# The first idle products of TensorE: 30 of 192 columns in place of 11 of 512

## The chip, the cores and the metric

The kernel runs on one core of a Trainium2 chip. That core has a matrix engine (TensorE, "PE" in the profile, with its weight loads shown apart as "PEld"), a vector engine (DVE), a scalar engine (ACT), GpSimd (POOL) and a sync engine (SP) that only issues transfers. Each engine works through its own stream of instructions; they meet through semaphores. Transfers run on 16 DMA engines. The metric is the device time of one execution in microseconds (us), lower is better.

## The reference

An attention with a decaying state is followed by a two-layer network with the exact GELU. Cut to what matters:

```python
# q, k, v: (4, 8, 768, 64); lam: (8,), one decay for each head
for b in range(nb):                       # blocks of 64 positions
    intra = einsum('bhic,bhjc->bhij', qb, kb) * Dmask[None]
    intra = einsum('bhij,bhjd->bhid', intra, vb)
    inter = einsum('bhid,bhde->bhie', qb * lam_pow[None], kv_state)
    out[:, :, sl] = intra + inter
    kv_state = lam_block * kv_state + einsum('bhsd,bhse->bhde', kb * rev_pow, vb)
...
x = out.transpose(0, 2, 1, 3).reshape(3072, 512)
h = x @ w_in                              # 512 -> 2048
g = 0.5 * h * (1.0 + erf(h / sqrt(2)))
result = g @ w_out                        # 2048 -> 512
```

## The kernel before

The 3072 tokens are worked on in 24 chunks of 128 positions (six positions of the sequence times four batches), and the network in six groups of four chunks, 512 tokens each. All products are in bfloat16 with float32 sums.

The order of TensorE's work is written out by hand. The kernel first issues all constants, loads and the start of the attention. Then a loop over the six groups issues the network's blocks (`mlp_blocks`), and a sorted list of due times (`todo`) places the attention's steps for later chunks between these blocks. So TensorE's stream is one fixed sequence without loops: every product stands in it as a pair of instructions, a weight load and a matmul, and there are 2619 such pairs.

In that sequence two kinds of stretches alternate. The network's blocks have long products: L518 (the first layer, up to 512 columns), L414 (the second layer, done by sums of halves as in Strassen's scheme, 256 columns) and, in the first group, L531. Between them lie the visits to the attention (`pair_visit`): `begin_answers` (L314, the states), `ask` (L279, scores), `ask_products` (L290, new state products), `end_answers` (L326 values, and L314 again). A visit has products of 64x64 with 64 columns, up to 128 of them in a row. What they need (transposed q and k) comes by DMA transposes that SP issues. The scaling of a visit's output to the network's input `x_t` is done on the vector engine at L333, and the next block of L518 waits for that.

At the very start TensorE has no data. GpSimd issues the loads of k, q and v of the first chunks; the weight columns come through SP. Until k is there, TensorE is given idle products: `keep_warm(n, new, cols)` (L576 to L581) multiplies a zero tile `idle` (memset at L107) by itself n times into a PSUM bank that nobody reads. Each is a weight load of 128 columns and a matmul over `cols` columns. The first call, in the line that the change touches (L595), stands before the first chunk's transposes (L166 in `transposed`); more calls, of 2 to 7 products of 256 columns, stand between the first steps, up to product 120 or so.

Of the kernel before, what the change touches and what calls it, by code (L numbers as in the profile page):

```python
# [15 lines left out]
def kernel(  # L16
# [131 lines left out]
    def bank(shape, dtype, tag, name):  # L148
        return ps.tile(shape, dtype, tag=tag, name=name, bufs=2 if tag in ("sc", "mh", "mo") else 1)
# [426 lines left out]
    def keep_warm(n, new=True, cols=256):  # L576

        if new:
            idle_ps[0] = bank([128, 512], F32, "mo", "idle_ps")
        for _ in range(n):  # L580
            nc.tensor.matmul(idle_ps[0][:, :cols], idle[:, :128], idle[:, :cols], start=True, stop=True)  # L581

    def early(n):
        live[n] = begin(n, early=True)
        return live[n]
# [6 lines left out]
    nc.scalar.copy(w_in_t[:, :, :256], wide_w)  # L592
    make_powers()
    nc.scalar.activation(warm, pos, ACT.Gelu)
    keep_warm(11, cols=512)  # L595
    c = early(0)
    causal(0)
    transposed(c, "k", "mh", copy)
# [266 lines left out]
```

## Time and profile before

| | us |
|---|---|
| median of three runs | 203.96 |
| lowest, highest | 203.42, 206.22 |
| the profiled execution's own time | 203.09 |
| its span (first to last instruction) | 201.3 |
| TensorE busy | 192.3 |
| VectorE / ScalarE / GpSimd busy | 122.5 / 82.7 / 111.3 |

The span is that of the profiled execution; its own time holds 1.8 us more, which lie outside the program's instructions. The page gives TensorE's products at L581 as one group, with the shapes of 512 and 256 columns together:

```profile
L581 PE MATMUL idle_ps<-idle 128*128 128x256 bf16 (+1 forms) x39 | 9.0, 366 | 1.2 <-DVE idle L107 1.2
```

Of these 39 products, 11 are of the first call. Columns of such a row: line, engine, operation, output and inputs, shape, count, then busy us and mean ns of one, then the engine's idle time just before them and what ended it. In the timeline the columns are start, duration, engine, line, operation, and in brackets the idle time before with its releaser; "issue" stands where the engine waited for nothing that the profile shows. In the view of windows they are the stretch, its length, the busy time with the count of instructions that ran in it, the granted clock, the DMA share and GB/s.

### The profile page before, as it was taken

Reading aid. Unit: us, or ns where it says so; the run is one execution under the profiler, and the core shown is the slowest. Engines: PE = TensorE matmul, PEld = TensorE weight load, DVE = VectorE, ACT = ScalarE, POOL = GpSimd, SP = SyncE. Lnnn points to the kernel's source line nnn. Section 1 sums busy time; section 2 is a strip of 40 time slices with the busy share of each in tenths; the row PEclk is TensorE's granted clock in tenths of the full one; section 3 lists DMA queues with packets and bytes.
Section 4 is the critical chain, followed back from the end, with each engine's and each line's share of the span. In section 5 each row is a group of like instructions: output and inputs, shape, how many; then the busy total and the mean of one; then the engine's idle time right before and its main releaser. Section 6 shows DMA issues by size and latency. Waiting matters only on the chain.

```text
span 201.3 us, 5976 instructions
## 1 busy us (share of the span) xinstructions
PE 192.3 (96%) x2619; PEld 141.6 (70%) x2619; DVE 122.5 (61%) x206; ACT 82.7 (41%) x149; POOL 111.3 (55%) x136
## 2 busy tenths in 40 slices
PE   7699999999999999799999999999999999999992
PEld 2378674555884788686488885588884788865881
DVE  3753507863674869594949678649639358341482
ACT  4964564324567313155620164520265510566200
POOL 8999973789968899992592299394400000000000
PEclk9999999999999999999999999999999999999998
DMA  5999999999999999999599779999930001400014
GB/s 113 155 174 176 198 207 200 156 216 152 145 207 136 137 146 134 141 272 145 61 98 140 234 53 118 102 66 115 155 142 3 3 0 61 151 0 3 0 52 156
DMA packets 102761, 24.76 MB, mean 123 GB/s; under 512 B 93264, under 2 KB 99920, under 8 KB 102736
## 3 DMA queue, kind: packets, MB, share of 16 engines
q0 software_dynamic: 81072, 13.38, 100.3%
q1 hardware_dynamic: 21664, 11.02, 27.7%
q8 instruction: 20, 0.33, 0.7%
q14 instruction: 5, 0.04, 0.1%
HBM read 27.27 MB, written 6.29 MB: 167 GB/s over the span
## 4 chain that ended last, share of the span: by engine, by line
PE 58%; DMA 19%; POOL 15%; DVE 4%; issue 2%; POOLq 0%; DVEq 0%
PE h_ps L518 28%; PE r_ps L414 8%; PE p_ps L414 7%; PE q_ps L414 7%; DMA q_t<-in_q_dram 5%; DMA v_t<-in_v_dram 5%; DMA w_out_t<-in_moe_w_out_dram 5%; DMA qT<-q_t 4%; POOL k_t L70 4%; PE s_ps L414 3%; POOL v_dec L160 3%; POOL v_t L70 3%; POOL w_in_t L94 3%; POOL q_t L70 3%; PE o_ps L314 2%
## 5 line engine op out<-in xcount | busy, mean ns | idle before, releaser
L521 ACT ACTIVATE g_t<-h_ps 128x512 bf16<-128x512 f32 (+2 forms) x99 | 57.8, 584 | 73.0 <-PE h_ps L518 73.0
L518 PE MATMUL h_ps<-x_t,w_in_t 128*128 128x256 bf16 (+3 forms) x640 | 87.7, 294 | 0.0
L518 PEld LDWEIGHTS <-w_in_t 128*128 128x128 bf16 x640 | 57.0, 98 | 24.7 <-DVE x_t L333 0.2
L389 DVE TENSOR_TENSOR g_sum<-g_t 128x1024 bf16<-128x1024 bf16 x50 | 34.7, 739 | 15.3 <-ACT g_t L521 15.3
L414 PEld LDWEIGHTS <-g_sum 128*128 128x128 bf16 x400 | 39.0, 98 | 5.1 <-issue 0.5
L160 POOL TENSOR_TENSOR v_dec<-v_t,lam_m 128x512 bf16<-128x512 bf16 x23 | 24.9, 1100 | 27.4 <-PE o_ps L326 16.9
L70 POOL DMA_DIRECT2D v_t<-in_v_dram x24 | 22.1, 919 | 2.2 <-DMA w_out_t<-in_moe_w_out_dram 1.7
L414 PE MATMUL r_ps<-w_sum,g_sum 128*128 128x256 bf16 x160 | 19.1, 272 | 0.3 <-DVE f_x L484 0.3
L73 POOL DMA_DIRECT2D k_t<-in_k_dram x24 | 18.6, 789 | 0.0
L73 POOL DMA_DIRECT2D q_t<-in_q_dram x24 | 18.2, 778 | 0.0
L414 PEld LDWEIGHTS <-g_t 128*128 128x128 bf16 x160 | 15.7, 98 | 2.9
L531 PE MATMUL o_ps<-w_out_t,g_t 128*128 128x512 bf16 x64 | 15.1, 380 | 0.0
L333 DVE TENSOR_TENSOR x_t<-o_ps,lam_q 128x512 bf16<-128x512 f32 x16 | 10.6, 685 | 5.0 <-PE o_ps L314 5.0
L70 POOL DMA_DIRECT2D q_t<-in_q_dram x12 | 10.8, 903 | 2.3 <-DMA w_out_t<-in_moe_w_out_dram 2.3
L70 POOL DMA_DIRECT2D k_t<-in_k_dram x12 | 11.1, 923 | 1.9 <-DMA w_out_t<-in_moe_w_out_dram 1.6
L305 DVE TENSOR_TENSOR sc_m<-sc_ps,cmask_d 128x512 bf16<-128x512 f32 x16 | 10.3, 681 | 0.0
L531 PEld LDWEIGHTS <-g_t 128*128 128x128 bf16 x64 | 5.8, 98 | 6.2
L581 PE MATMUL idle_ps<-idle 128*128 128x256 bf16 (+1 forms) x39 | 9.0, 366 | 1.2 <-DVE idle L107 1.2
L452 DVE TENSOR_TENSOR o_sb<-f_e,p_ps 128x512 f32<-128x512 f32 x5 | 3.4, 687 | 11.0 <-issue 11.0
L414 PE MATMUL p_ps<-w_out_t,g_sum 128*128 128x256 bf16 x80 | 9.6, 273 | 0.0
L414 PE MATMUL p_ps<-w_sum,g_t 128*128 128x256 bf16 x80 | 9.6, 273 | 0.0
L414 PE MATMUL q_ps<-w_sum,g_t 128*128 128x256 bf16 x80 | 9.6, 273 | 0.0
(90 smaller groups left out, 194.2 us busy)
## 6 DMA issues: line engine op xcount, KB each, us to landing
out_dram<-o_sb SPq DMA_DIRECT2D x9, 512.0 KB, 4.5
v_t<-in_v_dram POOLq DMA_DIRECT2D x24, 128.0 KB, 6.0
w_out_t<-in_moe_w_out_dram POOLq DMA_DIRECT2D x4, 512.0 KB, 10.2
w_in_t<-in_moe_w_in_dram POOLq DMA_DIRECT2D x7, 256.0 KB, 7.4
k_t<-in_k_dram POOLq DMA_DIRECT2D x12, 128.0 KB, 6.5
q_t<-in_q_dram POOLq DMA_DIRECT2D x12, 128.0 KB, 6.9
k_t<-in_k_dram POOLq DMA_DIRECT2D x24, 64.0 KB, 4.8
q_t<-in_q_dram POOLq DMA_DIRECT2D x24, 64.0 KB, 5.0
```

Source lines behind the costliest of these rows:

```text
L70: nc.gpsimd.dma_start(raw[n, name], chunk_of(name, n))
L73: nc.gpsimd.dma_start(raw[n, name][:, r::2, :], chunk_of(name, n)[:, r * HP:(r + 1) * HP, :])
L94: nc.gpsimd.dma_start(w_in_t[:, :, f], w_in_r[:, :, f])
L160: eng.tensor_mul(c.v_dec, c.v, lam_m[:, :, None].to_broadcast((128, H, D)))
L305: nc.vector.tensor_mul(w.sc_m[:, hi], w.sc_ps[hi], cmask_d[:, None, None, :].to_broadcast((128, 2, HP, D)))
L333: nc.vector.tensor_mul(x[:, :, :, HALVES[t]], pairs[n].o_ps[t], lam_q[:, :, None, HALVES[t]].to_broadcast((128, HP, 2, D)))
L389: nc.vector.tensor_tensor(gsum[i][:, ks, :], g_t[:, ka + k:ka + k + n4, ta], g_t[:, kb + k:kb + k + n4, tb], op=op)
L414: nc.tensor.matmul(o, left[i](k, slice(u * C, (u + 1) * C)), right[i](k), start=(begin and k == 0), stop=(k == KH - 1), skip_group_check=True)
L518: nc.tensor.matmul(h_ps[:, k, :], w_in_t[:, ki, (kf + k) * 128:(kf + k + 1) * 128], x_t[:, ki, cols], start=(k == 0 and ki == 0), stop=(ki ...
L521: nc.scalar.activation(g_t[:, kf:kf + ks, cols], h_ps, ACT.Gelu)
L531: nc.tensor.matmul(om[io], g_t[:, kf, io * C:(io + 1) * C], w_out_t[:, kf, :], start=(kf == 0), stop=(kf == NK2 - 1))
L581: nc.tensor.matmul(idle_ps[0][:, :cols], idle[:, :128], idle[:, :cols], start=True, stop=True)
```

## The change

One line: the first call of `keep_warm` issues 30 products of 192 columns in place of 11 of 512. That is 5760 columns in place of 5632, and 60 instructions in place of 22. The zero tile, the PSUM bank and the other calls stay as they are; so do the other engines' instructions, every wait and every transfer.

```diff
     make_powers()
     nc.scalar.activation(warm, pos, ACT.Gelu)
-    keep_warm(11, cols=512)
+    keep_warm(30, cols=192)
     c = early(0)
     causal(0)
     transposed(c, "k", "mh", copy)
```

## The prediction

> **What bounds the kernel now.** I began with the page, its span and busy times:
>
> ```profile
> span 201.3 us, 5976 instructions
> ...
> PE 192.3 (96%) x2619; PEld 141.6 (70%) x2619; DVE 122.5 (61%) x206; ACT 82.7 (41%) x149; POOL 111.3 (55%) x136
> ...
> q8 instruction: 20, 0.33, 0.7%
> ```
>
> TensorE is busy for 192.3 of 201.3 us and nothing else comes near, so the time can only change through its idle time, its clock or its amount of work. The work at stake is the idle products, which compute nothing that is used. The last row is for later: 20 packets carry TensorE's instructions while it runs, 0.33 MB / 20 = 16.4 KB each. TensorE issues 2 x 2619 = 5238 instructions (each product has a weight load), which is 262 for each packet.
>
> Second, the list of all waits of TensorE:
>
> ```profile
> PE o_ps L314 <- issue: 1.3, 2, 1.1
> PE idle_ps L581 <- DVE idle L107: 1.2, 1, 1.2
> PE t_ps L166 <- DMA k_t<-in_k_dram: 1.0, 2, 0.8
> PE t_ps L166 <- DMA q_t<-in_q_dram: 0.4, 2, 0.2
> PE r_ps L414 <- DVE f_x L484: 0.3, 1, 0.3
> PE sc_ps L189 <- DVE qT L169: 0.3, 1, 0.3
> PE sc_ps L279 <- DMA qT<-q_t: 0.3, 1, 0.3
> ```
>
> Two things are to be seen. The first real product (L166, a transpose of k) waits 0.8 us for its load, so the idle products in front of it end early. And the longest entry has no releaser at all: "issue" at L314, two pauses deep inside the kernel, 1.3 us in total.
>
> Third, the timeline, at the start (TensorE and its weight loads), and with it the view of the idle tile, restricted to the first 6 us (durations are ns, min/median/max):
>
> ```profile
> 1.19 4.57 PE L581 MATMUL idle_ps<-idle 128*128 128x512 bf16 x11 [1.19 <-DVE idle L107]
> 1.60 0.15 PEld L581 LDWEIGHTS <-idle 128*128 128x128 bf16 x1 [0.28 <-issue]
> ...
> 5.01 0.15 PEld L581 LDWEIGHTS <-idle 128*128 128x128 bf16 x1 [0.28 <-issue]
> 6.61 0.40 PE L166 MATMUL t_ps<-ident,k_t 128*128 128x128 bf16 x4 [0.85 <-DMA k_t<-in_k_dram]
> ...
> L581 PE MATMUL idle_ps<-idle x11: 380/634/634, 1.2 to 5.4; 128*128 128x512 bf16 x11
> ```
>
> From 1.60 to 5.01 lie eight steps of 0.426 us, one product of 512 columns each, so 0.83 ns a column. Only the last product, at 5.4, has the short duration, 380 ns in place of 634: TensorE runs slowly for its first 4 us and reaches its full rate near 5.3 us, while the idle products still run. They are there for that. They end at 5.76 and k arrives for 6.61.
>
> **The change at its own place.** It removes 11 products of 512 columns (11 x 0.426 = 4.69 us at the slow rate) and adds 30 of 192: 192 x 0.83 = 0.160 us each, 4.80 us in all. The difference of 0.11 us, even with every product slow, ends the group near 6.0 in place of 5.76 as the latest, and the wait for k (0.85 us) hides it: I cost it at nothing. If that cover were gone it would cost its 0.11 us. The bounds: no less than nothing, since k's load sets 6.61 whatever TensorE does; at most, a weight load (0.15 us in the rows above) might no longer lie beside a product. Then a product costs 0.31 us until 5.3 (13 of them) and, with half of 0.16 for the fast rate, about 0.23 after that (17 of them, 3.9 us): the group would end near 9.3, 2.7 us late. I take nothing, because each load in the rows starts beside a running product, and 0.15 still fits into 0.160. Total columns and their time being alike, I also leave the moment of full rate at about 5.3.
>
> **What the change moves.** The 19 extra products with their loads are 38 more instructions at the head of TensorE's stream; every later instruction of it stands 38 places further back. No other engine's stream, no wait and no DMA changes. So the places matter where the stream itself is brought in. Here are the two pauses of "issue", and the window counts (x is the number of products started since 0):
>
> ```profile
> 84.18 0.19 PE L314 MATMUL o_ps<-qT,state 64*64 64x64 bf16 x1
> 85.51 0.19 PE L314 MATMUL o_ps<-qT,mid 64*64 64x64 bf16 x1 [1.14 <-issue]
> ...
> 121.77 0.21 PE L314 MATMUL o_ps<-qT,mid 64*64 64x64 bf16 x1
> 122.14 0.19 PE L314 MATMUL o_ps<-qT,state 64*64 64x64 bf16 x1 [0.17 <-issue]
> ```
>
> ```profile
> 0.00:80.05 80.05, 76.21 (x971) 1.00 1.95 166
> 0.00:82.80 82.80, 78.95 (x995) 1.00 1.96 166
> 0.00:84.40 84.40, 80.52 (x1118) 1.00 1.96 165
> 0.00:113.50 113.50, 108.51 (x1483) 1.00 1.84 160
> 0.00:117.15 117.15, 112.16 (x1611) 1.00 1.80 161
> 0.00:119.20 119.20, 114.21 (x1630) 1.00 1.78 159
> 0.00:122.00 122.00, 116.99 (x1757) 1.00 1.77 157
> ```
>
> The pauses come after product 1118 and after product 1757. That is 639 products or 1278 instructions apart, five times 255.6, while a packet carries at most 262. I read this as blocks of 256 instructions (128 products), with an edge after product 1118 and after every 128th on either side, and both pauses as TensorE standing at an edge whose next block has not come. The DMA view of narrow windows (0.2 us in 40 slices of 5 ns; the tall number in the GB/s row is the packet's start) shows the packets, from windows that begin at 83.0, 119.1, 114.9 and 89.9:
>
> ```profile
> GB/s 154 154 462 154 256 282 155 410 180 154 384 230 103 334 154 103 130 107 130 3456 78 206 102 154 78 53 78 128 77 102 102 102 102 128 77 77 102 128 128 154
> q8 instruction: 1, 0.02, 33.2%
> ...
> GB/s 51 26 77 51 102 51 51 128 51 77 26 128 102 102 102 102 102 77 3379 128 51 102 102 128 26 128 77 128 77 102 102 128 77 77 102 128 102 51 128 102
> q8 instruction: 1, 0.02, 47.6%
> ...
> GB/s 410 410 410 0 410 0 1229 1229 0 410 410 410 0 0 3277 410 819 410 410 0 0 0 819 1638 0 410 410 410 0 410 0 0 410 410 410 819 0 0 0 1229
> q8 instruction: 1, 0.02, 47.2%
> ...
> GB/s 410 410 410 819 819 461 435 410 819 410 410 410 0 0 0 410 410 0 410 4096 819 410 410 0 0 410 436 845 0 819 0 410 410 0 410 819 819 410 410 0
> q8 instruction: 1, 0.02, 29.1%
> ```
>
> They start at 83.10, 119.19, 114.97 and 90.00; a share of 16 engines over 0.2 us gives their lengths, 1.06, 1.52, 1.51 and 0.93 us. So the first packet ends at 84.16 and TensorE goes on at 85.51, 1.35 us later; the second ends at 120.71 and TensorE goes on at 122.14, 1.43 us later. Two unlike pauses, one lag: that ties each to its packet.
>
> Why just there? A block seems to be fetched when the stream enters the one before it. The edge before product 1118 is product 990, near 82.25 (five products of L518, some 0.11 us each, before 82.80), and between lies a dense run: 123 products from 82.80 to 84.18, 0.011 us each. From edge to next edge TensorE needs only 1.9 us, and the block took 85.51 - 82.25 = 3.3 us. At the second pause the edge is product 1629, near 119.1, and the block took 122.14 - 119.1 = 3.0 us. Moreover TensorE reached the first of these edges late, held by the vector engine:
>
> ```profile
> 81.86 0.77 PEld L518 LDWEIGHTS <-w_in_t 128*128 128x128 bf16 x8 [0.17 <-DVE x_t L333]
> ```
>
> After the change every edge falls 19 of these products earlier:
> - The edges around the first pause become products 971 (80.06) and 1099 (84.18 - 19 x 0.011 = 83.97). That is 3.9 us for a block that took 3.3: no pause. Gain 85.51 - 84.18 less one step of 0.011, 1.32 us.
> - Around the second they become 1610 (117.05, from the row of 1611 at 117.15) and 1738 (121.56). 4.5 us for a block that took 3.0: no pause. Gain 122.14 - 121.77 less a step, 0.36 us.
> - A third pair comes close: 1482 (113.49) and 1610 (117.05), 3.56 us apart. The same edge of before, 1501 near 113.65, had its packet at 114.97, 1.51 us long; with a lag of 1.4 the block was usable at 117.88, and nobody needed it before 119.1. Moved with its edge it is usable at 117.72 and TensorE stands for 0.67 us. By the blocks of 3.0 to 3.3 us it would not stand at all. I take 0.67, since that row is of the same place with the same transfers around it.
>
> Sum: -1.32 - 0.36 + 0.67 = -1.0 us, with -1.7 as the lower end. What is late next? No other wait of TensorE between 85.51 and 121.77 is in the list of waits, so I expect the time to stay won.
>
> The Trainium skill, "Runtime: NRT & Kernel Launch", section "Instruction fetch mechanics", says that an engine's instructions are refilled in 16 KiB blocks of 256 instructions, the next fetched while the current one runs, and that crossing a block's edge is "mostly hidden". The block size agrees with the 16.4 KB above; "hidden" does not agree with pauses of 1.32 and 0.36 us. By that rule the shift would be worth nothing and the sum would be 0.
>
> **Rivals.**
> *No change.* The pauses come from something that doesn't move with the stream (a wait that the profile doesn't show), or new edges pause as much. For it: "issue" names no cause, and 1278 is two short of five times 256. Against: the equal lag behind two packets. The time stays that of the profiled execution, 203.1. Chance 0.14; the skill's rule of hidden fetches ends here too.
>
> *Slower: a block that comes late in heavier DMA traffic.* The edge at 85.51 (product 1118) had its packet only at 90.00, usable 1.35 us after its end at 90.93, so 6.8 us after its edge. If the block asked for at 80.06 took as long, TensorE would stand 6.8 - 3.9 = 2.9 us where it now stands 1.32: the sum is 2.9 - 1.32 - 0.36 + 0.67 = +1.9 us, time 205.0. It decides from 3.9 + 1.32 = 5.2 us on. Against it: the stream runs somewhat ahead of TensorE, and product 971 lies ahead of the hold at 81.86, so the request should come sooner, not later. Chance 0.13.
>
> *Clock.* The full rate comes only in the next dense stretch. What that costs:
>
> ```profile
> 6.50:8.70 2.20, 1.55 (x21) 1.00 2.42 154
> 8.70:12.10 3.40, 3.07 (x46) 1.00 2.00 167
> ```
>
> TensorE has 4.62 us of fast work in this stretch; at half rate the 5.5 us from 6.61 to 12.1 do 2.75 us of it, so 1.9 us are lost, 204.0 with the gain of 1.0. For it: 0.11 us more of idle products is no guard, and one of the three times of before is 206.22. Against it: the busy stretch is as long as before. The skill's "TensorE: Matmul & The Clock Gate", Part 1, speaks of a free-running window of 3.4 us, by which both kernels would draw this lot alike; one trace can't show that. Chance 0.11. The weight load that no longer fits beside its product (+2.7, less the gain: 204.8) gets 0.02.
>
> **The numbers.** The forecast has chance 0.60. The profiled execution's own time is 203.09 (span 201.3 and 1.8 around it), which gives 202.1; the median of the runs shown, 203.96, lies 0.87 above it, and from there the same sum gives 203.0. I say 202.5. Low: 203.09 - 1.7 = 201.4, taken as 201.3. High: 205.2, which takes in both slower rivals at 204.0 to 205.0 and the no-change case; two of these mishaps together lie above it. Two per cent, 4.1 us, is about what a measurement of this kernel can tell from no change. Faster by that (under 199.9) would need more idle time than the waits of TensorE after 6.61 hold (some 2.7 us together): 0.04. Slower by that (over 208.0) needs two of the mishaps on top of the median, or a far longer slow start: 0.07. Within: 0.89.
>
> **What would show it.** In the profile after: L581 with 30 products at about 0.16 us steps, L166 still waiting for k at about 6.6; no "issue" pause near 84 and 122, counted in products 1137 and 1776; one new pause of up to 0.7 us near 116, after product 1629; the span 200.3. It is wrong if pauses stay at the same products of the dense runs (then the blocks aren't the cause), if a pause of over 1.3 us stands near 84 (then the block's way is slower than I think), or if products after 6.6 still have slow steps (then the clock).

## The result, and the profile after

The changed kernel takes 202.11 us (median of 20 runs) against 204.22 us of the kernel before beside it (20 runs): ratio 0.9909, 95% interval 0.9887 to 0.993, some 1.9 us faster. By the bound of two per cent that is no difference; by its own interval it is one. The profiled execution took 201.49 us, with a span of 199.7 us against 201.3. Ratios here and below leave out an execution over 1.5% above the fastest of its kernel; the times beside them are medians of all.

The page of the changed kernel, its span and busy times, and then the list of TensorE's waits:

```profile
span 199.7 us, 6002 instructions
...
PE 190.8 (96%) x2626; PEld 143.4 (72%) x2638; DVE 121.5 (61%) x206; ACT 82.8 (41%) x149; POOL 111.2 (56%) x136
```

```profile
PE idle_ps L581 <- DVE idle L107: 1.2, 1, 1.2
PE t_ps L166 <- DMA k_t<-in_k_dram: 1.1, 2, 0.9
PE t_ps L166 <- DMA q_t<-in_q_dram: 0.9, 3, 0.5
PE h_ps L518 <- issue: 0.3, 1, 0.3
PE o_ps L531 <- issue: 0.3, 2, 0.2
PE sc_ps L189 <- DVE qT L169: 0.3, 1, 0.3
PE h_ps L518 <- DMA w_in_t<-in_moe_w_in_dram: 0.2, 1, 0.2
```

The entry "o_ps L314 <- issue" of before is gone: neither pause is left. The products of this trace (2626) are 12 fewer than its weight loads (2638), which are complete; the two waits of L531 are the holes of such missing records. So I count weight loads from here on. A load runs one ahead of its product: the first pause of before stands after load 1119.

The pause of L518 is real. The timeline around it, the window count up to it, and the DMA view of the window from 113.5 to 113.7:

```profile
115.15 0.49 PE L518 MATMUL h_ps<-x_t,w_in_t 128*128 128x256 bf16 x3
115.98 0.28 PE L518 MATMUL h_ps<-x_t,w_in_t 128*128 128x256 bf16 x1 [0.34 <-issue]
...
0.00:115.80 115.80, 81.77 (x1630) 1.00 1.75 162
...
GB/s 410 819 1229 410 0 0 410 0 0 819 0 0 0 819 819 0 0 3686 410 0 0 410 410 410 0 410 0 410 0 819 410 410 819 819 410 0 410 0 410 0
q8 instruction: 1, 0.02, 27.4%
```

It stands after load 1630, which to within one is the third edge of the prediction (product 1629). Its packet starts in the 18th slice, at 113.585, is 0.88 us long and ends at 114.46; TensorE goes on at 115.98, 1.52 us later.

At the start the two groups compare as foretold:

```profile
1.19 4.28 PE L581 MATMUL idle_ps<-idle 128*128 128x192 bf16 x30 [1.19 <-DVE idle L107]
6.42 0.40 PE L166 MATMUL t_ps<-ident,k_t 128*128 128x128 bf16 x4 [0.94 <-DMA k_t<-in_k_dram]
...
L581 PE MATMUL idle_ps<-idle x30: 246/364/364, 1.2 to 5.2; 128*128 128x192 bf16 x30
```

Thirty products end at 5.47, and TensorE waits 0.94 us for k. The full rate came near 4.6 us here, where the prediction had left it at 5.3: 22 products had begun by 4.60 and 27 by 5.00.

### The profile page after: what moved, and what is told of

Read it like the earlier page. It is cut to its first block, busy times and chain, and to the rows that moved or that the text cites. A ratio compares the mean times of both kernels' runs of the same rounds, so it can differ in the third digit from the quotient of the medians.

```text
span 199.7 us, 6002 instructions
## 1 busy us (share of the span) xinstructions
PE 190.8 (96%) x2626; PEld 143.4 (72%) x2638; DVE 121.5 (61%) x206; ACT 82.8 (41%) x149; POOL 111.2 (56%) x136
## 4 chain that ended last, share of the span: by engine, by line
PE 77%; DMA 10%; POOL 10%; issue 1%; DVE 0%; POOLq 0%
PE h_ps L518 35%; PE r_ps L414 9%; PE p_ps L414 9%; PE q_ps L414 9%; DMA q_t<-in_q_dram 6%; PE s_ps L414 4%; DMA w_out_t<-in_moe_w_out_dram 4%; PE o_ps L531 3%; POOL w_in_t L94 3%; POOL k_t L70 2%; POOL q_t L70 2%; PE o_ps L314 2%; POOL v_t L70 2%; POOL v_dec L160 1%; PE o_ps L326 1%; PE kv_ps L290 1%
## 5 line engine op out<-in xcount | busy, mean ns | idle before, releaser
L518 PE MATMUL h_ps<-x_t,w_in_t 128*128 128x256 bf16 (+3 forms) x632 | 87.5, 293 | 0.9 <-issue 0.3
L518 PEld LDWEIGHTS <-w_in_t 128*128 128x128 bf16 x640 | 57.0, 98 | 25.5 <-DVE sc_m L305 0.6
L389 DVE TENSOR_TENSOR g_sum<-g_t 128x1024 bf16<-128x1024 bf16 x50 | 33.8, 720 | 16.2 <-ACT g_t L521 16.2
L531 PE MATMUL o_ps<-w_out_t,g_t 128*128 128x512 bf16 x60 | 14.6, 379 | 0.4 <-issue 0.3
L531 PEld LDWEIGHTS <-g_t 128*128 128x128 bf16 x64 | 5.9, 98 | 6.2
L581 PE MATMUL idle_ps<-idle 128*128 128x192 bf16 (+1 forms) x58 | 8.7, 303 | 1.2 <-DVE idle L107 1.2
L414 PE MATMUL s_ps<-w_sum,g_sum 128*128 128x256 bf16 x80 | 9.6, 273 | 0.0
```

Of the source, the lines that this page charges most:

```text
L389: nc.vector.tensor_tensor(gsum[i][:, ks, :], g_t[:, ka + k:ka + k + n4, ta], g_t[:, kb + k:kb + k + n4, tb], op=op)
L414: nc.tensor.matmul(o, left[i](k, slice(u * C, (u + 1) * C)), right[i](k), start=(begin and k == 0), stop=(k == KH - 1), skip_group_check=True)
L518: nc.tensor.matmul(h_ps[:, k, :], w_in_t[:, ki, (kf + k) * 128:(kf + k + 1) * 128], x_t[:, ki, cols], start=(k == 0 and ki == 0), stop=(ki ...
L531: nc.tensor.matmul(om[io], g_t[:, kf, io * C:(io + 1) * C], w_out_t[:, kf, :], start=(kf == 0), stop=(kf == NK2 - 1))
```

## The experiments

Two theories stood against each other. **Blocks**: the time follows where the edges of 128 products fall in the work. **Shape**: it follows what the first idle products are, by their own time or by the clock. The first four runs part them: one moves the stream without the shape, one has the shape without moving, one moves it the other way, one moves it far.

**Moved only.** The first call stays 11 of 512; later calls issue twice as many products of half the width.

```diff
     transposed(c, "k", "mh", copy)
-    keep_warm(3, new=False)
+    keep_warm(6, new=False, cols=128)
     transposed(c, "q", "mo", copy)
     causal(1)
-    keep_warm(2)
+    keep_warm(4, cols=128)
...
-        1: [lambda: keep_warm(7), lambda: outputs(live[1])],
+        1: [lambda: keep_warm(14, cols=128), lambda: outputs(live[1])],
```

> The first idle products as before (11 of 512); the stream moved by the same 19 products by splitting 19 later idle products of 256 columns into two of 128 each, so the columns stay. Theory (blocks of 256 instructions): as the changed kernel, ratio to before 0.991 (0.986 to 0.996); no pause near 84 and 122 us, one of 0.2 to 0.7 us near 116 after product 1629. Rival (the shape of the first idle products, by the clock or their own time): as before, ratio 1.00, with pauses of about 1.3 and 0.4 us at the same work as before.

Measured: ratio 0.9919 (0.9886 to 0.9951), 201.76 us. Its list of waits has no "issue" entry at all; the pauses near 84 and 122 are gone, and the third, expected with 0.2 to 0.7 us, is not there either. The gain is there without the changed line.

**Shape only.** The first call as 23 of 245 columns, and later calls with products merged into 512 columns, so that the count ahead of the work is that of before (the edit is shown against the kernel before).

```diff
-    keep_warm(11, cols=512)
+    keep_warm(23, cols=245)
...
-    keep_warm(3, new=False)
+    keep_warm(1, new=False, cols=512)
+    keep_warm(1, new=False)
...
-        4: [lambda: scores(live[2]), lambda: keep_warm(7)],
+        4: [lambda: scores(live[2]), lambda: keep_warm(3, cols=512), lambda: keep_warm(1, new=False)],
```

> The first idle products as 23 of 245 columns (the change's kind of shape), the stream not moved: 12 products fewer later, where idle products of 256 columns are merged into products of 512. Theory (blocks): as before, ratio 1.00 (0.996 to 1.005), with pauses of about 1.3 us near 84 and 0.4 us near 122, after products 1118 and 1757. Rival (shape): as the changed kernel, 0.991, without pauses there.

Measured: ratio 1.0017 (0.9988 to 1.0046), 203.73 us: the shape brings nothing. Its profile, of an execution of 206.72 us that the ratio doesn't hold, can't stand for that time: there TensorE waits 2.6 us at L484 (last section), and no pause follows at the edge behind it. That this kernel still has the pauses of before thus rests on its time alone.

**Moved back.** The first call as before, the later calls merged as in the run above: 12 products fewer.

> The first idle products as before (11 of 512), the stream 12 products shorter ahead of all the work, by the same merging of later idle products. Theory (blocks): the edges fall 12 products later in the work, so from edge to edge TensorE needs only about 1.4 us near 84 and 1.5 near 121 in place of 2.0 and 2.6; the pauses grow to about 1.9 and 1.4 us, ratio 1.008 (1.003 to 1.012), again after products 1118 and 1757 or so of its own count, which is other work. Rival (shape): 1.00.

Measured: ratio 1.0002 (0.9971 to 1.0032): not the 1.008 expected, and this interval leaves 1.008 out. The places came true, in a profiled execution of 205.58 us that the ratio doesn't hold. The rows after each pause, and the load counts up to them:

```profile
87.75 0.49 PE L518 MATMUL h_ps<-x_t,w_in_t 128*128 128x256 bf16 x3 [1.48 <-issue]
124.78 0.19 PE L314 MATMUL o_ps<-qT,state 64*64 64x64 bf16 x1 [1.14 <-issue]
...
0.00:87.00 87.00, 54.64 (x1119) 1.00 1.93 170
0.00:124.20 124.20, 83.33 (x1758) 1.00 1.76 155
```

Loads 1119 and 1758 again, in work that lies 12 products later: the first pause is now at L518, after the dense run, where before it was at L314 inside it. They last 1.48 and 1.14 us, not 1.9 and 1.4. The executions in the ratio lose less than I worked out; why isn't shown, since none of them has a profile. The ratio also leaves out five of the twelve, 204.95 to 206.34 us, at a granted clock of 0.997 to 1.0. The median of all twelve is 204.28 us, that of all executions of before 203.48. So this run shows where the edges stand, and leaves open what they cost.

**Moved by 59.** The first call as 42 of 134 columns, all later ones split as in the first run.

> The first idle products as 42 of 134 columns, all 28 later ones split into two of 128: the stream moved by 59 products. Theory (blocks): no pauses near 84 and 121; new ones in two other dense runs, about 2 us near 93 after product 1374 of its own count and 0.3 to 1 us near 113 after product 1630; together 2.3 to 3.0 us against the 1.7 of before, ratio 1.004 (1.000 to 1.008). Rival (more and shorter idle products help by themselves): at most the 0.991 of the change, with no pause at 93.

Measured: ratio 1.0131 (1.007 to 1.0191), 207.4 us, worse than expected. The rows after the two pauses in its profile (of an execution of 208.31 us that the ratio doesn't hold), the counts up to them, and the packet of the longer one (window 94.4 to 94.6):

```profile
76.33 0.38 PE L414 MATMUL q_ps<-w_out_t,g_sum 128*128 128x256 bf16 x2 [1.48 <-issue]
97.46 0.61 PE L518 MATMUL h_ps<-x_t,w_in_t 128*128 128x512 bf16 x1 [3.21 <-issue]
...
0.00:75.60 75.60, 50.65 (x991) 1.00 2.02 169
0.00:96.00 96.00, 65.54 (x1374) 1.00 2.04 170
...
GB/s 128 179 128 154 179 179 179 128 102 179 230 102 179 128 179 128 154 179 154 179 129 77 179 128 27 3457 78 77 102 78 128 26 77 27 51 53 26 26 51 26
q8 instruction: 1, 0.02, 44.0%
```

Both follow, to within one, a multiple of 128 counted from 1118: 990 (loads one ahead) and 1374. The pause at 1374 was foretold; that at 990 was not, and the one at 113 did not come. The packet starts at 94.52, when TensorE, busy until 94.25, has already stopped; it ends at 95.93, and TensorE goes on at 97.46: 1.53 us. The half clock behind it, shown in the last section, cost this execution some 2.9 us more (an estimate, half of the 5.8 us there); the executions in the ratio have no profile.

**Moved by 16**, to save the third pause: `keep_warm(27, cols=211)`.

> The first idle products as 27 of 211 columns: the stream moved by 16 products in place of 19. Theory (blocks): the third edge falls three products of L518 later, some 0.3 us, which is the pause that the changed kernel still has near 116 (0.34); the first pair of edges stays 3.6 us apart against a block of 2.5 to 3.3. So no pause over 0.15 us at any edge, ratio to before 0.989 (0.985 to 0.994). Rival (the pauses near 84 come back already here): 0.993 or more, with a pause near 84 after product 1118.

Measured: ratio 0.9916 (0.9893 to 0.9939), not told apart from the change; the 0.989 expected lies just outside the interval. In its profile there is no pause at any edge, as expected, but a wait of 1.4 us at L484 that has nothing to do with edges.

**Thin idle products**: `keep_warm(30, cols=32)`, 960 idle columns.

> The first idle products as 30 of 32 columns: the stream as in the changed kernel, but only 960 idle columns, so that TensorE is idle for some 2 us more before k comes. The gain by the edges stays. Theory of the prediction's rival on the clock: the full rate comes only in the dense stretch up to about 12 us, 1.9 us are lost, ratio 1.000 (0.995 to 1.006), with slow steps of L581 and L518 after 6.6 us. If the idle products' length doesn't matter: 0.991 and fast steps from 6.6 us on.

Measured: ratio 0.994 (0.9919 to 0.9961). The clock part came true, its price did not. Timeline of its start, then weight loads issued up to 16 and 43.5 us, for this kernel:

```profile
1.19 0.98 PE L581 MATMUL idle_ps<-idle 128*128 128x32 bf16 x30 [1.19 <-DVE idle L107]
6.41 0.61 PE L166 MATMUL t_ps<-ident,k_t 128*128 128x128 bf16 x4 [4.23 <-DMA k_t<-in_k_dram]
...
0.00:16.00 16.00, 7.91 (x131) 1.00 1.60 150
0.00:43.50 43.50, 25.62 (x436) 1.00 1.71 173
```

and for the changed kernel:

```profile
0.00:16.00 16.00, 10.14 (x151) 1.00 1.59 151
0.00:43.50 43.50, 26.87 (x438) 1.00 1.68 175
```

The four transposes from 6.41 last 0.61 us in place of 0.40: the slow rate, though the column of the granted clock reads 1.00 there. It lasts until some 12.7 us: two idle products of 256 columns take 0.61 us in the row at 11.74 and 0.39 in that at 12.78. At 16 us the kernel is 20 products or 1.4 us behind (the changed one had begun load 131 by 14.6), at 43.5 us two. Between, the changed kernel waits 0.16 us for `w_in` (at 18.03) and 0.51 for q (at 41.25); the thin one, coming later, has neither wait in its list. So most of what a slow start costs is taken back at the loads of the first 43 us.

**Both once more**, for a second profile of each.

> The kernel before once more, for a second profile of it. Theory (blocks): a pause of 1.0 to 1.8 us near 84 after product 1118 and one of 0.2 to 0.8 us near 122 after product 1757, each ending 1.3 to 1.5 us after its instruction packet. Rival (the pauses are an accident of one execution): none there.

> The changed kernel once more. Theory (blocks): no pause at products 1118 and 1757 of its own count, at most 0.7 us after product 1629. Rival: pauses of about 1.3 us anywhere near 84 or 122.

Measured: 204.75 and 201.87 us, one run each. Before has a pause near 87, after load 1119, of 1.7 us; the one near 122 is missing, which I had not expected. The changed kernel has no pause at any edge, not even after 1629. The row and the count of before:

```profile
87.44 0.19 PE L314 MATMUL o_ps<-qT,mid 64*64 64x64 bf16 x1 [1.71 <-issue]
...
0.00:86.50 86.50, 54.74 (x1119) 1.00 1.97 162
```

**Values later.** The other wait that changes from profile to profile is L484. This kernel is the changed one with GpSimd's scaled values of chunks 12 and 13 after the next two loads of k.

```diff
-          (1 + 0.56, decayed, n + M, n + M + 1), (1 + 0.56, prefetch, 4 * M), (1 + 26 * B, decayed, n + M + 2, n + M + 3),
+          (1 + 0.56, key_first, n + M, n + M + 1), (1 + 26 * B, decayed, n + M + 2, n + M + 3),
...
+    def key_first(*chunks):
+        m = next_load[0]
+        assert m == 4 * M
+        load(m, "k")
+        decayed(*chunks)
+        load(m, "q")
+        load(m, "v")
+        next_load[0] += 1
```

> The changed kernel with one more edit on GpSimd: the scaled values of chunks 12 and 13 (the two L160 products near 79 us) are made after the two k loads of chunk 16 in place of before them, some 1.5 us later. Theory (the wait at L484, 0.3 to 2.6 us in the profiles so far, comes from the vector engine's g_sum at L389 being stretched while GpSimd's L160 runs beside it): all g_sum products near 74 to 80 take 0.7 us, no wait of r_ps for L484 over 0.1 us, time 0 to 1.4 us below the changed kernel, ratio to before 0.987 (0.983 to 0.992). Rival (the stretch is an accident of its own, or the values now come too late for L290): 0.991 or more, with a wait at L290 or L326 near 83.

> The changed kernel on the same chip, to stand beside the one with the values later: ratio to before 0.991 (0.988 to 0.994), no pause at the two places of before, up to 0.7 us after product 1629; g_sum near 79 stretched to between 0.7 and 3 us.

Measured: 0.99 (0.9864 to 0.9935), 201.64 us, and beside it the changed kernel alone 0.9918 (0.9889 to 0.9946), 201.67 us: not told apart. The 0.987 expected lies inside the interval, and so does no gain at all. The vector engine's and GpSimd's rows of the timeline, first of the changed kernel in this call, with the wait that follows on TensorE:

```profile
78.09 1.46 DVE L389 TENSOR_TENSOR g_sum<-g_t 128x1024 bf16<-128x1024 bf16 x1
79.07 2.39 POOL L160 TENSOR_TENSOR v_dec<-v_t,lam_m 128x512 bf16<-128x512 bf16 x2
80.20 0.49 PE L414 MATMUL r_ps<-w_sum,g_sum 128*128 128x256 bf16 x3 [0.71 <-DVE f_x L484]
```

and of the one with the values later:

```profile
78.89 0.68 DVE L389 TENSOR_TENSOR g_sum<-g_t 128x1024 bf16<-128x1024 bf16 x1
81.19 2.19 POOL L160 TENSOR_TENSOR v_dec<-v_t,lam_m 128x512 bf16<-128x512 bf16 x2
```

Beside GpSimd's products the sum takes 1.46 us, away from them 0.68, and the wait at L484 is gone. The cause is supported, by one profile of each; a gain in time is not shown. What sets the stretch isn't clear from the rows: at 0.68 us it would have ended at 78.77, before the recorded start of the products, and in the first profile of the changed kernel it takes 0.77 us (from 78.36) though the products start at 78.65. Nothing that was tried beats the change clearly.

## Why the prediction was right

- *The change at its own place costs nothing.* Right. The products step at 0.14 us on average (30 starts from 1.2 to 5.2), since the full rate came earlier than assumed; TensorE waits 0.94 us for k behind them, and the shape alone gave 1.0017.
- *The stream moves by 38 instructions, and the edges with it.* Right, and shown from both sides: moving alone gives 0.9919, the shape alone nothing. The prediction left one doubt, 1278 instructions being two short of five times 256. The trace settles it: between the two pauses TensorE also has two semaphore instructions, which the count of products leaves out. The row is from the view of L279 in before, from 85.4 to 122 (PEldq is TensorE's sequencer):

```profile
L279 PEldq EVENT_SEMAPHORE  x2: 51/51/51, 93.7 to 120.8; - x2
```

- *The two pauses go.* Right in all three profiles of the changed kernel, and in those of the four other kernels moved by 16 or 19. The 1.32 and 0.36 us are what they cost in one execution of before; the second profile has 1.7 and none.
- *A third pause after product 1629, 0.67 us.* Right in place, too large: 0.34 in the first profile, none in the second, 0.3 in the third. In the first its packet was 0.88 us long where I had taken the 1.51 us of before. This is a mis-sized term.
- *Sum -1.0 us.* The profiled pair gives -1.6: the edges -1.32 - 0.36 + 0.34 = -1.34, and the rest in small waits, some less (k 0.19 us earlier, 0.34 at L484, 0.28 for qT), some more (0.5 at the loads of q, 0.2 for `w_in`); these come and go between executions. The ratio gives -1.9 (1.4 to 2.3), more than the profiled pair. How the rest of the gap is made up isn't settled. So the mechanism was right, and the gain was taken at about half of what the ratio gives. That the forecast of 202.5 us still lies 0.4 from the 202.11 is partly luck: from the median the same sum gave 203.0, and starting partly from a profiled execution that was quicker than most made up for a gain taken too small.
- *Late blocks.* The rival's mechanism exists: the block at 1374 in the kernel moved by 59. It did not strike the changed kernel, but by little. In its first profile the packet for the edge at 1118 starts at 80.33 and is 1.33 us long; with a lag of 1.4 us the block was there near 83.1, by estimate, and TensorE began load 1119 after 83.53.
- *Clock.* The forced slow start lasts as long as I thought, yet it costs some 0.4 to 0.6 us (0.994 against 0.991 to 0.992, with overlapping intervals), not 1.9: it puts TensorE back by 1.4 us, and the loads take most of that up.
- *Hidden edges.* The Trainium skill, "Runtime: NRT & Kernel Launch", section "Instruction fetch mechanics", calls the crossing of a block's edge mostly hidden. Of some 20 edges in a run no profile here lists a pause at more than two, and half of the profiles list none; those listed have idle times of 0.2 to 3.2 us.

## What to carry to other kernels

When TensorE pauses with no releaser in a run of short products, count its instructions up to the pause, weight loads and semaphore instructions with them: if pauses stand at multiples of 256 from each other, the stream itself is the first suspect. Moving it without any other change, as here, is the test. Then the number of instructions ahead is a knob: split or merge products that cost nothing, and look where the edges fall against the dense runs, which here use up a block in 2 us. Such a gain belongs to one stream only, and any later edit that adds or removes an instruction ahead moves it again.

## What was not expected of the hardware

*The lag behind an instruction packet is nearly constant*: 1.35 and 1.43 us in the two pauses of before, 1.52 after, 1.53 in the kernel moved by 59, and 1.29 to 1.48 in the five other pauses at an edge that the profiles list. What differs is when the packet starts and how long it is (0.88 to 1.85 us at these pauses).

*A pause can cost the clock.* The kernel moved by 59 around its long pause, in windows (the column after the count is the granted clock):

```profile
94.25:97.40 3.15, 0.00 (x0) 0.86 0.60 63
97.50:103.30 5.80, 5.80 (x14) 0.50 1.43 108
103.40:110.00 6.60, 6.60 (x52) 1.00 1.33 124
```

After 3.2 us without a product the clock is at half for some 6 us of work: 14 products of 512 columns in 5.8 us, 0.41 us each. In the profile of the shape-only kernel a wait of 2.6 us did the same, for 3.4 us (the waits of 1.8 and 1.5 us in the moved-back kernel did not):

```profile
83.32 0.92 PE L414 MATMUL r_ps<-w_sum,g_sum 128*128 128x256 bf16 x7 [2.59 <-DVE f_x L484]
...
84.50:87.90 3.40, 3.40 (x39) 0.50 3.06 109
```

*A sum on the vector engine is held beside GpSimd.* That wait came from one sum of two operands in SBUF, while GpSimd made its values:

```profile
79.33 3.34 DVE L389 TENSOR_TENSOR g_sum<-g_t 128x1024 bf16<-128x1024 bf16 x1
79.94 2.17 POOL L160 TENSOR_TENSOR v_dec<-v_t,lam_m 128x512 bf16<-128x512 bf16 x2
```

3.34 us in place of 0.68, ending 0.56 us after GpSimd's second product. The Trainium skill, "SBUF — State Buffer", section "Who interferes with whom", says that a vector instruction with two SBUF inputs contends with a GpSimd instruction that reads SBUF; these rows and those of the values made later agree. The size of it varies, from 0.77 to 3.34 us for this sum in the profiles shown or named here.
